# Strassen output projection of a gated MLP: when a sum, a load and a weight part take their turn

## The chip, the core and the metric

The kernel runs on one core of a Trainium2 chip. The core has five engines that each work through their own instructions in order: PE (matrix products; PEld is its loading of the stationary operand), DVE (elementwise work), ACT (activation functions and copies), POOL and SP. In the part of the kernel that matters here SP does nothing but issue DMA transfers between the chip's memory (HBM) and the on-chip memory (SBUF). An instruction waits on semaphores of other engines or of DMAs, and everything behind it on its engine waits with it.

The metric is the device time of one execution in microseconds (us), the median of several.

## The reference

One input x of 2048 tokens by 576 features goes through a layer norm and then two branches, and the result is `x + s * silu(B)`:

```python
xn = _layernorm(x)
s = _A_ref(xn, wqkv, wo)          # sliding-window attention, 32 heads, window 256
# B: a gated MLP with a mixing of tokens
z  = gelu(xn @ w_in)              # 2048 x 4608, split into z1 and z2
z2 = _layernorm(z2)
g  = w_sp @ z2 + b_sp             # 2048 x 2048 times 2048 x 2304
B  = (z1 * g) @ w_out             # 2048 x 2304 times 2304 x 576
return x + s * silu(B)
```

Everything is float32. The change lies in the last line but one, the product `(z1 * g) @ w_out`, and in what closes it (`silu`, the product with s, the sum with x, the store).

## The kernel before

The kernel first does the layer norm, the attention, `s` and z1, z2, then the big product with `w_sp`, and at about 1652 us of its span begins the product with `w_out`. This last part is called the output stage here.

**Halves.** A float32 product is made of three passes: each operand is halved into a high part, a copy in the type fp32r (`act.activation(hi, src, Copy)`, line 115, on ACT), and a low part, what is left (`dve.tensor_tensor(lo, src, hi, subtract)`, line 116, on DVE). The passes are high times high, high times low, low times high. So a product can begin when the high half is there, and its third matmul needs the low half. The helper is `split`.

**Tiles.** The left matrix y = z1 * g, kept transposed in memory as `y_d` (2304 x 2048), is cut into four quadrant blocks a11, a12, a21, a22: first index for the token half, second for the feature half. A row pair p (0 to 7) takes 128 tokens of each token half; one block is 1152 features x 128 tokens, a tile of 128 x 1152, loaded from `y_d` in one DMA of 576 KB. The four blocks have fixed places: a11 and a21 in the tile `zr`, a22 and a12 in the tile `u2` (the profile writes it `u`). Blocks of the next pair are loaded over those of this one once their last reader is done.

**Products.** Pair 0 is computed plainly (`first_pair`: four blocks, two products each, 216 matmuls). Pairs 1 to 7 use Strassen's scheme in Winograd's form, seven products of 27 matmuls (128 x 288 out of 128 x 128 blocks): P1 = a11 B11, P2 = a12 B21, P3 on what is left in a12 with B22, P4 = a22 with the weight sum T4, P5 on the sum in a22 with T1, P6 on the sum in a11 with T2, P7 on the sum in a21 with T3. The list `SEQ` has the order: P4 P1 P6 P2 P5 P7 for pair 1, and then, pair by pair, P4, P1, P3 of the pair before, P6, P2, P5, P7.

**Operand sums.** Four sums in place, on DVE, make the Winograd operands. They are called A to D here: A, line 1325, a22 = a21 + a22; B, line 1326, a21 = a11 - a21; C, line 1328, a11 = a22 - a11; D, line 1330, a12 = a12 - a11. `y_form` halves the block of a product into one of three operand tiles `o0`, `o1`, `o2` and then runs the sums that belong there: A and B behind P4's block, C behind P1's, D behind P2's.

**Turns.** After product i `formed(i + 3)` halves the operand of product i + 3, whose tile product i has just left free, and `y_load` fetches a block of the next pair over it where that block is no longer read: a11 behind P2, a22 behind P5, a21 behind P7, a12 behind P3. A pair's result is closed twice, behind P7 and behind P3, by `finish`: `sv = sv * silu`, `xr = xr + sv` (lines 1500 and 1501), the store of `xr` to `out`, and then `load_end`, which loads the rows of s (`sv`) and of x (`xr`) for the next closing. Each of these has one buffer, so the next `xr` is loaded when the store has read the last one to its end.

**Weights.** `w_out` has 63 blocks of 128 x 288 for the scheme (B11, B21, B22, B12, T4, T2, T1, nine each), in 13 tiles of five. `w_fetch(i)` loads part i (720 KB; two loads where a tile spans two of the matrices), `w_halve(i)` halves it. Parts 0 to 6 come before the stage, 7 to 12 (tiles b5, w0, w1, w2, w3, w4; w4 has three blocks) in its first products. T3 is put where B12 was, in three parts (`t3_fetch`, `t3_halve`), since pair 0 needs B12 and no other T3. Raw parts lie in two buffers `wr` in turn.

**The start.** While pair 0 runs, the last gate products z1 * g (six multiplications, line 1358, and six stores to `y_d`, 256 KB each) are run off from a list called `lazy`; the memory they used (`wk`) is then closed and a new pool `yp` opened in it for w2 to w4, `sv`, `xr` and others, so these wait for the six stores.

**Order.** In this part the kernel is under a manual schedule: each engine's instructions stand in the order in which the code calls them. So the order of lines in the loop over `SEQ` is the order on SP, DVE and ACT.

Of the kernel before, what the change touches and what calls it, by code (L numbers as in the profile page):

```python
# [64 lines left out]
def kernel(  # L65
# [1142 lines left out]
    with ExitStack() as ph:  # L1208
# [108 lines left out]
        def y_form(i):  # L1317
            p, prod = SEQ[i]
            home = yw if i % 3 < 2 else homes["o2"]
            o = home.tile([P, 2304], F32R, name=f"o{i % 3}", bufs=1).rearrange("p (a f t) -> p a f t", a=2, t=P)  # L1320
            q = {name: quads.get((p, name)) for name in QUAD_AT}
            split(o[:, 0], o[:, 1], q[OF.get(prod, prod)])
            operands[p, prod] = o
            if prod == "P4":
                dve.tensor_tensor(q["a22"], q["a21"], q["a22"], ALU.add)
                dve.tensor_tensor(q["a21"], q["a11"], q["a21"], ALU.subtract)
            if prod == "P1":
                dve.tensor_tensor(q["a11"], q["a22"], q["a11"], ALU.subtract)
            if prod == "P2":
                dve.tensor_tensor(q["a12"], q["a12"], q["a11"], ALU.subtract)  # L1330
# [155 lines left out]
        def load_end():  # L1486
            if row_order:
                r = end_rows(*row_order.pop(0))
                t = [yp.tile([P, D], F32, name=n, bufs=1) for n in ("sv", "xr", "gs")]
# [63 lines left out]
        def formed(i):  # L1553
            if i < len(SEQ):
# [3 lines left out]
                if p == 0 or (p < LAST and prod in after_):  # L1558
                    y_load(p + 1, prod if p == 0 else after_[prod])

        for i, (p, prod) in enumerate(SEQ):
            if p == 0:
                first_pair(i, prod)
                if i == 0:
                    w_halve(8, right, "w0")
                    w_fetch(9, right)
                    w_fetch(10, right)
                    y_load(1, "a12")
# [3 lines left out]
                    y_load(1, "a11")  # L1572
                    y_load(1, "a21")
                    load_end()
                    w_halve(9, right, "w1")
                formed(i + 3)
# [3 lines left out]
                if i == 1:  # L1580
                    w_fetch(11, right)
                    w_halve(10, yp, "w2")
                    finish()
                    w_fetch(12, right)
                    w_halve(11, yp, "w3")
                if i == 2:
                    t3_fetch(right, T3_PARTS[0])
                    w_halve(12, yp, "w4")
                if i == 3:
                    finish()  # L1590
                    t3_fetch(right, T3_PARTS[1])
                    t3_halve(T3_PARTS[0])
                    t3_fetch(right, T3_PARTS[2])
                    t3_halve(T3_PARTS[1])
                    t3_halve(T3_PARTS[2])
# [4 lines left out]
            formed(i + 3)  # L1600
            if prod in ("P7", "P3"):
# [77 lines left out]
```

## Time and profile before

| what | value |
|---|---|
| time of 3 runs | median 1920.37 us (1917.13 to 1921.77) |
| profiled execution | 1926.44 us, of which span 1924.4 us and 2.0 us around it |
| granted TensorE clock, mean of the span | 0.985 |
| PE busy in the span | 1844.4 us (96%) |
| DVE, ACT busy in the span | 1139.1 us (59%), 945.1 us (49%) |
| first matmul of the output stage to the end of the span | 1652.4 to 1924.4 us, 272 us |

The profiled execution is 6.1 us longer than the median of the runs; everything taken from the trace is in its time. The profile counts a matmul as busy to its modelled end, so PE's share says little; waits and the starts of matmuls say more. DMA issues stand under SP (written SPq): a row's time is that of the issue. When a transfer has landed is seen from what waited for it. In the rows `o` is an operand tile, `w` and `b` are weight tiles, `c` a PSUM bank of the output stage.

### The profile page before, as it was taken

The numbers are of one execution on the slowest core, as the hardware profiler recorded it, in microseconds if no ns is written. First come the engines' busy times: TensorE is split into PE (matmuls) and PEld (weight loads), VectorE is DVE, ScalarE is ACT, GpSimd is POOL, SyncE is SP. The second block draws the span as 40 slices with busy tenths as digits, with TensorE's granted clock in tenths as the row PEclk, the third lists the DMA queues.
The fourth block names the chain that finished last, engine by engine and source line by source line (L and its number), as shares of the span: only waits on it lengthen the run. The fifth ranks groups of instructions, "written<-read, shape, count | busy, mean of one in ns | idle before, by whom it ended". The sixth has DMA issues, their size and how long they took to land.

```text
span 1924.4 us, 38178 instructions
## 1 busy us (share of the span) xinstructions
PE 1844.4 (96%) x14363; PEld 1604.9 (83%) x14363; DVE 1139.1 (59%) x2289; ACT 945.1 (49%) x1758; POOL 432.2 (22%) x507
## 2 busy tenths in 40 slices
PE   8999999999999999999999999999999999969887
PEld 8999999997777677777988788888888888868887
DVE  6321334467666777632267877679765777456666
ACT  5432223325666576666476655555545444233232
POOL 3232333343555455554000000212000000000000
PEclk9999999999999999999999999999999999979999
DMA  7885698786666666646777777887775567733444
GB/s 254 200 233 147 228 306 287 261 256 184 171 189 182 158 187 187 183 124 198 248 253 243 233 243 238 294 297 258 258 251 179 187 200 255 238 116 121 138 125 123
DMA packets 266920, 405.75 MB, mean 211 GB/s; under 512 B 52336, under 2 KB 180592, under 8 KB 266608
## 3 DMA queue, kind: packets, MB, share of 16 engines
q1 hardware_dynamic: 266736, 403.32, 68.1%
q8 instruction: 113, 1.85, 0.4%
q14 instruction: 71, 0.58, 0.1%
HBM read 285.35 MB, written 117.09 MB: 209 GB/s over the span
## 4 chain that ended last, share of the span: by engine, by line
PE 69%; DMA 11%; DVE 11%; ACT 3%; SPq 3%; issue 2%; POOL 0%; DVEq 0%; ACTq 0%; POOLq 0%
PE acc L1428 31%; PE mb L206 11%; PE ma L671 6%; PE mb L671 5%; PE ops L752 4%; PE ma L206 4%; PE tps L724 3%; DMA u<-y_d 2%; PE sp L600 2%; DVE o L116 2%; SPq L363 1%; ACT o L115 1%; DMA s_d<-so 1%; DMA zr<-y_d 1%; DMA out_dram<-xr 1%
## 5 line engine op out<-in xcount | busy, mean ns | idle before, releaser
L1428 PE MATMUL acc<-spl,zh 128*128 128x512 f32 x1008 | 393.4, 390 | 2.3 <-DVE spl L116 2.0
L1428 PE MATMUL acc<-sph,zh 128*128 128x512 f32 x1008 | 393.0, 390 | 0.8 <-ACT sph L115 0.8
L1428 PE MATMUL acc<-sph,zl 128*128 128x512 f32 x1008 | 392.9, 390 | 0.0
L604 DVE CUSTOM_DVE_ANT_0 junk<-sp,band 128x384 bf16<-128x384 f32 (+1 forms) x512 | 276.2, 539 | 116.2 <-PE sp L600 30.2
L728 ACT ACTIVATE pt<-tps 128x384 f32<-128x384 f32 (+2 forms) x576 | 231.3, 441 | 122.8 <-PE tps L724 77.7
L116 DVE TENSOR_TENSOR spl<-spr,sph 128x1024 fp32r<-128x1024 f32 x168 | 208.7, 1242 | 39.6 <-ACT sph L115 38.6
L671 PE MATMUL mb<-b,z1wh 64*128 64x512 f32 x648 | 225.6, 401 | 2.7 <-ACT z1o L676 2.2
L671 PE MATMUL ma<-b,z1wh 64*128 64x512 f32 x648 | 224.8, 399 | 0.6 <-ACT zt L948 0.4
L1428 PEld LDWEIGHTS acc<-spl,zh 128*128 128x128 f32 x1008 | 189.4, 188 | 43.2 <-DVE spl L116 4.3
L1428 PEld LDWEIGHTS acc<-sph,zh 128*128 128x128 f32 x1008 | 189.3, 188 | 40.6 <-ACT sph L115 1.2
L1428 PEld LDWEIGHTS acc<-sph,zl 128*128 128x128 f32 x1008 | 189.4, 188 | 38.8
L1519 PE MATMUL c<-b,o 128*128 128x288 f32 x1056 | 158.5, 311 | 35.6 <-DVE o L116 23.1
L115 ACT ACTIVATE zh<-b 128x384 fp32r<-128x384 f32 x168 | 87.4, 520 | 208.0 <-PE acc L1428 205.2
L1519 PEld LDWEIGHTS c<-b,o 128*128 128x128 f32 x1056 | 152.4, 202 | 39.6 <-DVE o L116 26.4
L115 ACT ACTIVATE sph<-spr 128x1024 fp32r<-128x1024 f32 x168 | 176.0, 1048 | 14.0 <-DMA spr<-sc_d 8.6
L724 PE MATMUL tps<-att 56*128 56x384 f32 (+1 forms) x576 | 177.7, 346 | 2.4 <-DMA att<-mhl 1.8
L116 DVE TENSOR_TENSOR zl<-b,zh 128x384 fp32r<-128x384 f32 x168 | 100.8, 600 | 127.1 <-ACT zh L115 116.8
L600 PE MATMUL sp<-att 54*128 54x384 f32 (+1 forms) x512 | 162.0, 351 | 3.2 <-DVE mx L604 3.0
L671 PE MATMUL ma<-b,z1wl 64*128 64x512 f32 x324 | 128.4, 396 | 0.0
L671 PE MATMUL mb<-b,z1wl 64*128 64x512 f32 x324 | 128.0, 395 | 0.0
L949 DVE BATCH_NORM_STATS2 st<-zt 128x6 f32<-128x384 f32 x96 | 49.3, 548 | 131.3 <-ACT zt L948 131.0
L724 PEld LDWEIGHTS tps<-att 56*128 56x128 f32 x576 | 99.8, 184 | 31.0 <-issue 9.4
(214 smaller groups left out, 4206.8 us busy)
## 6 DMA issues: line engine op xcount, KB each, us to landing
spr<-sc_d SPq DMA_DIRECT2D x96, 512.0 KB
spr<-in_w_sp_dram SPq DMA_DIRECT2D x72, 512.0 KB
zr<-z_d SPq DMA_DIRECT2D x144, 192.0 KB
z_d<-zt SPq DMA_DIRECT2D x48, 384.0 KB
z_d<-z1o SPq DMA_DIRECT2D x72, 256.0 KB
z1t<-z_d SPq DMA_DIRECT2D x72, 256.0 KB
y_d<-z1t SPq DMA_DIRECT2D x72, 256.0 KB
a<-in_w_sp_dram SPq DMA_DIRECT2D x64, 256.0 KB
```

The lines of the kernel that those rows point to most:

```text
L115: act.activation(hi, src, AF.Copy)
L116: dve.tensor_tensor(lo, src, f32(hi), ALU.subtract)
L206: pe.matmul(banks[h][:, :n], *both[h][i], start=i == 0, stop=i == STEPS - 1)
L600: pe.matmul(ps[:, :w], q_of(u, j)[0:54, i * P:(i + 1) * P], k_of(u, j)[0:54, k0:k0 + w], start=True, stop=True)
L604: dve.tensor_tensor_reduce(out=junk[:, :w], in0=ps[:, :w], in1=band[:, m0:m0 + w], scale=1.0, scalar=-3.0e38, op0=ALU.add, op1=ALU.max, ac ...
L671: pe.matmul(ps, w, x_, start=n == 0, stop=n == STEPS - 1)
L724: pe.matmul(ps[:, :m * P], k_of(u, j)[:, (kb - base) * P:(kb - base + 1) * P], q_of(u, j)[:, (a - lo) * P:(a - lo + m) * P], start=True, s ...
L728: act.activation(pt[:, j, d0:d0 + n * P], ps[:, (qa - a) * P:(qa - a + n) * P], AF.Exp, scale=scale)
L752: pe.matmul(o_ps[c][32 * j:32 * j + 32, (qa - 4 * c) * P:(hi - 4 * c + 1) * P], vgs[u][:, kb - k0, j * VW:j * VW + 32], pt[:, j, (qa - kb) ...
L949: dve.bn_stats(st2[:, s, pc, :], zv)
L1428: pe.matmul(acc[j], z[:, ps], w[:, cs], start=s == i == 0 and n in OPENS, stop=s == 7 and i == 2, skip_group_check=True)
L1519: pe.matmul(banks[key][:, :288], y, w, start=begin and k == n == 0, stop=close and k == 8 and n == 2, skip_group_check=True)
```

## The change

- In `y_form` the sums A and B move from behind P4's low half to behind P1's low half, ahead of C.
- `xr` has two buffers instead of one.
- At the start, the loads of a11 and a21 of pair 1 move on SP from behind the six gate stores to ahead of weight part 9. Halving the operand of product 3 and the load of a22 of pair 1 move to ahead of the stores. Part 10 is fetched behind four of the stores, and a12 of pair 1 behind `sv` and `xr`. The halving of w1 goes behind that of product 3's operand.
- Halvings of weight parts and T3 parts each come one or more products later: w3 in product 2, w4 in product 3, the T3 parts behind products 5, 6 and 7.

The same instructions run, with the same shapes.

```diff
@@ y_form
-            if prod == "P4":
+            if prod == "P1":
                 dve.tensor_tensor(q["a22"], q["a21"], q["a22"], ALU.add)
                 dve.tensor_tensor(q["a21"], q["a11"], q["a21"], ALU.subtract)
-            if prod == "P1":
                 dve.tensor_tensor(q["a11"], q["a22"], q["a11"], ALU.subtract)
@@ load_end
-                t = [yp.tile([P, D], F32, name=n, bufs=1) for n in ("sv", "xr", "gs")]
+                t = [yp.tile([P, D], F32, name=n, bufs=1 + (n == "xr")) for n in ("sv", "xr", "gs")]
@@ formed
-                if p == 0 or (p < LAST and prod in after_):
-                    y_load(p + 1, prod if p == 0 else after_[prod])
+                if i == 3 or (p < LAST and prod in after_):
+                    y_load(p + 1, "a22" if i == 3 else after_[prod])
@@ the loop over SEQ, pair 0
                 if i == 0:
+                    y_load(1, "a11")
+                    y_load(1, "a21")
                     w_halve(8, right, "w0")
                     w_fetch(9, right)
+                formed(i + 3)
+                if i == 0:
+                    run_lazy(6)
+                    w_halve(9, right, "w1")
                     w_fetch(10, right)
-                    y_load(1, "a12")
                     run_lazy(len(lazy))
                     gates.close()
                     yp = open_pool(ph, "yp")
-                    y_load(1, "a11")
-                    y_load(1, "a21")
                     load_end()
-                    w_halve(9, right, "w1")
-                formed(i + 3)
+                    y_load(1, "a12")
...
                     finish()
+                if i == 2:
                     w_fetch(12, right)
                     w_halve(11, yp, "w3")
-                if i == 2:
                     t3_fetch(right, T3_PARTS[0])
-                    w_halve(12, yp, "w4")
                 if i == 3:
                     finish()
+                    w_halve(12, yp, "w4")
                     t3_fetch(right, T3_PARTS[1])
-                    t3_halve(T3_PARTS[0])
-                    t3_fetch(right, T3_PARTS[2])
-                    t3_halve(T3_PARTS[1])
-                    t3_halve(T3_PARTS[2])
                 continue
...
             formed(i + 3)
+            if i == 5:
+                t3_halve(T3_PARTS[0])
+                t3_fetch(right, T3_PARTS[2])
+            if i in (6, 7):
+                t3_halve(T3_PARTS[i - 5])
```

Two places show how the order on an engine changes. First SP at the start of the output stage, before; `wr` is a raw weight part (5x288 is a whole part; `4x288` and `288` are the two loads of part 10), `zr<-y_d` is a11 or a21 of pair 1, the first `u_15526<-y_d` a12 and the second a22:

```order
L1274 DMA wr<-t_d 128x5x288 x2
L1274 DMA wr<-t_d 128x4x288
L1274 DMA wr<-t_d 128x288
L1315 DMA u_15526<-y_d 128x9x128
L1364 DMA y_d<-z1t 128x512 x6
L1315 DMA zr<-y_d 128x9x128 x2
L1490 DMA sv<-s_d 128x576
L1491 DMA xr<-in_x_dram 128x576
L1315 DMA u_15526<-y_d 128x9x128
L1274 DMA wr<-t_d 128x5x288
```

And with the change, where the first `u_15526<-y_d` is a22 and the second a12:

```order
L1274 DMA wr<-t_d 128x5x288
L1315 DMA zr<-y_d 128x9x128 x2
L1274 DMA wr<-t_d 128x5x288
L1315 DMA u_15526<-y_d 128x9x128
L1363 DMA y_d<-z1t 128x512 x4
L1274 DMA wr<-t_d 128x4x288
L1274 DMA wr<-t_d 128x288
L1363 DMA y_d<-z1t 128x512 x2
L1489 DMA sv<-s_d 128x576
L1490 DMA xr<-in_x_dram 128x576
L1315 DMA u_15526<-y_d 128x9x128
L1274 DMA wr<-t_d 128x5x288
```

a11 and a21 pass part 9, part 10, a12 and six stores; a22 passes part 10, six stores, `sv` and `xr`; a12 falls behind all of these.

Second, DVE at the turn of a pair, before; `o<-u` is the low half of P4's block, `o<-zr` that of P1's, `u3s` the first of the three small sums behind P7:

```order
L116 TENSOR_TENSOR o_22110<-u_15526,o_22110 128x1152
L1325 TENSOR_TENSOR u_15526<-zr,u_15526 128x1152
L1326 TENSOR_TENSOR zr<-zr 128x1152
L116 TENSOR_TENSOR o_22143<-zr,o_22143 128x1152
L1328 TENSOR_TENSOR zr<-u_15526,zr 128x1152
L1539 TENSOR_TENSOR u3s<-c_22049,t_22000 128x288
```

And with the change:

```order
L116 TENSOR_TENSOR o_22110<-u_15526,o_22110 128x1152
L116 TENSOR_TENSOR o_22141<-zr,o_22141 128x1152
L1325 TENSOR_TENSOR u_15526<-zr,u_15526 128x1152
L1326 TENSOR_TENSOR zr<-zr 128x1152
L1327 TENSOR_TENSOR zr<-u_15526,zr 128x1152
L1538 TENSOR_TENSOR u3s<-c_22049,t_22000 128x288
```

The low half of P1 stands ahead of A and B instead of behind them; the three sums A, B, C still stand ahead of `u3s`. (Line numbers of the changed kernel are one lower up to the loop over `SEQ`.)

## The prediction

> **What bounds the kernel now.** I read the table by stages first, then PE's waits in the output stage, then the instructions of each engine in time, to see who is late for whom. The waits, from 1490 us to the end:
>
> ```profile
> PE c L1519 <- DVE o L116: 26.2, 17, 4.3
> PE c L1519 <- ACT o L115: 8.8, 3, 5.6
> PE c L1519 <- ACT t L1534: 6.1, 1, 6.1
> ```
>
> PE loses 41.1 us to late operand halves, all behind 1681 us; the big product before them waits for next to nothing and is untouched. They come in two kinds. PE at the start of the stage:
>
> ```profile
> 1652.39 28.75 PE L1519 MATMUL c<-b,o 128*128 128x288 f32 x216
> 1686.76 0.85 PE L1519 MATMUL c<-b,o 128*128 128x288 f32 x2 [5.61 <-ACT o L115]
> ...
> 1696.80 3.58 PE L1519 MATMUL c<-b,o 128*128 128x288 f32 x25 [2.99 <-DVE o L116]
> 1702.85 0.85 PE L1519 MATMUL c<-w,o 128*128 128x288 f32 x2 [2.47 <-ACT o L115]
> 1704.25 5.83 PE L1519 MATMUL c<-w,o 128*128 128x288 f32 x25 [0.55 <-DVE o L116]
> 1716.18 0.85 PE L1519 MATMUL c<-b,o 128*128 128x288 f32 x2 [6.11 <-ACT t L1534]
> ...
> 1723.36 3.73 PE L1519 MATMUL c<-w,o 128*128 128x288 f32 x27
> 1726.92 5.31 PE L1519 MATMUL c<-b,o 128*128 128x288 f32 x39
> 1732.07 2.15 PE L1519 MATMUL c<-w,o 128*128 128x288 f32 x15
> ```
>
> From 1723.36 to 1726.92 an undisturbed product takes 3.56 us. Pair 0 (28.75) ends at 1681.14; six products of pair 1 and P4 of pair 2 would be through 7 x 3.56 later, at 1706.1. They were through at about 1734.1: 28 us lost, some 18 in waits and 10 in slow matmuls (25 of them in 5.83 us instead of 3.58).
>
> Why the first wait: ACT stood 18 us for a22 of pair 1, whose load SP issued only at 1677.33, behind weights, stores and the other blocks; it landed 8.2 us later, in a stretch in which the DMAs were full.
>
> ```profile
> 1677.33 0.38 SPq L1315 DMA_DIRECT2D u<-y_d  x1
> ...
> 1685.54 1.16 ACT L115 ACTIVATE o<-u 128x1152 fp32r<-128x1152 f32 x1 [18.18 <-DMA u<-y_d]
> ```
>
> The same stretch in the table by stages (last columns: granted clock, DMA share, GB/s):
>
> ```profile
> 1660.00:1668.00 8.00, 8.00 (x62) 8.00 (x62) 7.23 (x10) 3.03 (x3) 0.00 (x0) 1.00 0.59 183
> 1668.00:1676.00 8.00, 8.00 (x63) 8.00 (x62) 1.26 (x1) 0.00 (x0) 0.00 (x0) 1.00 1.00 318
> 1676.00:1684.00 8.00, 5.14 (x39) 4.91 (x38) 0.00 (x0) 0.00 (x0) 0.00 (x0) 1.00 1.10 318
> ```
>
> At 1660 to 1668 the DMAs were 0.59 busy, DVE nearly full; then the DMAs were full and DVE and ACT empty.
>
> From pair 2 on there is a rhythm. DVE from one turn of pairs to the next:
>
> ```profile
> 1791.26 1.36 DVE L1325 TENSOR_TENSOR u<-zr,u 128x1152 f32<-128x1152 f32 x1 [3.10 <-DMA zr<-y_d]
> ...
> 1796.59 0.45 DVE L1539 TENSOR_TENSOR u3s<-c,t 128x288 f32<-128x288 f32 x1
> ...
> 1799.59 1.36 DVE L116 TENSOR_TENSOR o<-u,o 128x1152 fp32r<-128x1152 f32 x1 [1.56 <-ACT o L115]
> ...
> 1811.22 1.36 DVE L116 TENSOR_TENSOR o<-u,o 128x1152 fp32r<-128x1152 f32 x1 [1.57 <-ACT o L115]
> ...
> 1814.33 1.35 DVE L116 TENSOR_TENSOR o<-zr,o 128x1152 fp32r<-128x1152 f32 x1
> 1818.24 1.36 DVE L116 TENSOR_TENSOR o<-u,o 128x1152 fp32r<-128x1152 f32 x1 [2.57 <-ACT o L115]
> 1822.67 1.36 DVE L1325 TENSOR_TENSOR u<-zr,u 128x1152 f32<-128x1152 f32 x1 [3.07 <-DMA zr<-y_d]
> 1824.07 1.36 DVE L1326 TENSOR_TENSOR zr<-zr 128x1152 f32<-128x1152 f32 x1
> 1825.34 1.35 DVE L116 TENSOR_TENSOR o<-zr,o 128x1152 fp32r<-128x1152 f32 x1
> 1826.73 1.36 DVE L1328 TENSOR_TENSOR zr<-u,zr 128x1152 f32<-128x1152 f32 x1
> 1828.01 0.45 DVE L1539 TENSOR_TENSOR u3s<-c,t 128x288 f32<-128x288 f32 x1
> ```
>
> The low halves are those of P3 (1799.59), P2, P5, P7, P4 (1818.24) and P1 (1825.34). SP and ACT beside it:
>
> ```profile
> 1800.98 0.37 SPq L1315 DMA_DIRECT2D u<-y_d  x1
> ...
> 1805.34 1.17 ACT L115 ACTIVATE o<-u 128x1152 fp32r<-128x1152 f32 x1 [3.24 <-DMA u<-y_d]
> ...
> 1812.61 0.37 SPq L1315 DMA_DIRECT2D u<-y_d  x1
> 1814.07 0.35 SPq L1502 DMA_DIRECT2D out_dram<-xr  x1
> ...
> 1817.70 0.33 SPq L1491 DMA_DIRECT2D xr<-in_x_dram  x1
> 1818.09 0.43 SPq L1315 DMA_DIRECT2D zr<-y_d  x1
> ```
>
> and SP's waits of this kind, summed (us, times, longest):
>
> ```profile
> SPq L1491 <- DMA out_dram<-xr: 36.2, 15, 3.8
> ```
>
> Followed link by link this is a closed loop in which PE has no part: u3s 1796.59, its SiLU, P3's halves, the load of a12 (issued 1800.98, landed 1805.34), P2's halves, D, the sum and SiLU behind P3, P5's halves (low 1811.22), the closing of a pair, the store of `out`, the wait of 3.2 us for it in front of `xr`, the load of a21 behind that (issued 1818.09, landed 1822.6), A, B, P1's low half, C, u3s at 1828.01. It takes 31.42 us, while seven products need 7 x 3.56 = 24.9. PE's waits of 3.2 us at P1 and its slow matmuls there only fill the difference. First and last turn of this kind:
>
> ```profile
> 1733.67 0.45 DVE L1539 TENSOR_TENSOR u3s<-c,t 128x288 f32<-128x288 f32 x1
> ...
> 1891.99 0.45 DVE L1539 TENSOR_TENSOR u3s<-c,t 128x288 f32<-128x288 f32 x1
> ```
>
> Five rounds, 158.3 us, 31.66 each.
>
> **The loop after the change.** With a second `xr` buffer the load of `xr` no longer waits for the store, so a21 can be issued as soon as P7's low half is through: 1814.33 + 1.35, say 1815.7 instead of 1818.09. At the same 4.54 us it lands at 1820.2. That wait hides another: the load of a22 (1812.61) lands at 1817.05, then P4's low half begins at 1818.24. What is late next is this path. Behind P4's low half now stands P1's (1.28 later, by the pitch 1826.73 to 1828.01), then A at 1820.8; a21 is there 0.6 us earlier. A and B take 1.39 each (1824.07 less 1822.67), C 1.28: u3s at 1824.85. The round is 28.26 instead of 31.42, 3.16 less: 1.87 since A begins earlier, 1.28 since the low half is out from between A and u3s. Behind A, B and C on DVE wait u3s, P3's low half and P6's; they gain the 3.16 with them. P1's low half itself comes 5.8 us earlier (1819.52 against 1825.34), so PE's wait there goes; PE will wait at P3 instead, whose low half ends 4.4 us after u3s.
>
> Against 158.3 us five rounds of 28.26 are 141.3: **17.0 us**. The chain cannot be shorter unless its own members are. It can be longer: the transfer of `xr` (288 KB) now runs beside a22 and a21. I take 0.25 us for each of the loop's two loads, the spread of the rows here (4.36 to 4.54 us), five rounds: **minus 2.5**. Bound on the bad side: both loads at 1 us more, minus 10; on the good side nothing.
>
> **The start after the change.** a11 and a21 of pair 1 pass weight part 9 on SP, and with it all that stood ahead of them. This is what was in flight from 1652 to 1690 us:
>
> ```profile
> DMA packets 9138, 8.24 MB, mean 217 GB/s; under 512 B 304, under 2 KB 8112, under 8 KB 9136
> ```
>
> At the 318 GB/s of the full stretch it takes 25.9 us from the stage's begin, to 1678.3; the reordered start moves the same bytes. Part 11 (0.74 MB, 2.3 us) comes last; I take 1680.5 for it and 1676 for all before it. Then DVE's chain, step by step, with 1.28 to 1.36 for an operand half, 1.39 for a sum (rows above), 1.6 for a weight part:
>
> ```profile
> 1662.70 1.66 DVE L116 TENSOR_TENSOR w<-wr,w 128x1440 fp32r<-128x1440 f32 x1
> ```
>
> - w0's low half (this row) ends at 1664.3, that of product 3 now follows and ends at 1665.6: a22 is issued at 1665.7, 11.6 us earlier, and lands by 1673.9 even at 8.2 us. P4's halves end by 1676.5, wanted at 1681.1: the wait of 5.6 and the 0.55 behind it go, with 4.6 us to spare.
> - w2 (part 10, ACT 1.4, DVE 1.6) ends at 1679, the first closing at 1680.5, P1's low half at 1681.9 (wanted 1684.7: the 2.99 goes), A, B, C at 1686, w3 at 1687.6, P6's low half at 1689 (wanted 0.4 us sooner). This is what moving w3's and w4's parts behind the operands is worth: w3 no longer stands ahead of P1's half.
> - The next closing ends at 1690.5, w4 (three blocks, about 1.1) at 1691.6, P2's low half at 1693 (wanted 0.3 sooner), D at 1694.4, P5's at 1695.7 (in time). The 2.47 and 6.11 shrink to these tenths. The T3 parts, which stood ahead of P2's half, come behind P5's half and later ones, each beside a running product.
> - a22 of pair 2 is issued at 1695.8 and lands at 1700.2 (4.44 as at 1812.61); T3's first part, a small sum and P7's low half end at 1698.6, a21 lands at 1703.2; P4's low half ends at 1702.8, T3's last part at 1703.2, P1's low half at 1704.6, A, B, C at 1708.6. So the first turn's u3s falls at 1708.5 instead of 1733.67: **25.2 us**.
>
> PE alone would allow 28 (above), the bound on the good side; the 10 us of slow matmuls are in it, as they followed the waits. On the bad side w2, w3 and w4 each land 3.7 us later (8.2 against 4.5 us, what a22's load lost in the full stretch) and each holds the operand half behind it on ACT: 11 less, 14 us. I stay near the good end since from 1679 on DVE sets the steps, not the DMAs; for the forecast's own range I allow one part late, 21.5.
>
> **The end.** The last loads of `xr` wait for a store too; the last closing but one pays for it:
>
> ```profile
> 1919.43 0.46 DVE L1501 TENSOR_TENSOR xr<-xr,sv 128x288 f32<-128x288 f32 x1 [1.23 <-DMA xr<-in_x_dram]
> ```
>
> That goes: **1.2**.
>
> **Sum.** 17.0 - 2.5 + 25.2 + 1.2 = 40.9. The profiled execution had 1926.44 us (span 1924.4): 1885.5. The median is 6.1 lower, and nothing in the trace says where, so I take the same gain off it: 1920.37 - 40.9 = **1879.5**. Its own range by the bounds: at best 17 + 28 + 1.2 = 46, 1874; at worst 17 - 10 + 21.5 + 1.2 = 30, 1890.
>
> **Rivals.**
> 1. *PE becomes the bound by its clock.* Behind waits of 2.47 and 0.55 us, 25 matmuls took 5.83 us, but behind 2.99 only 3.58. In the new rhythm a wait of about 2.4 us remains at P3: P5 goes from 1812.6, P7, P4 and P1 follow to 1826.8, and P3's low half ends at 1824.85 + 4.36 = 1829.2. One slow product per round (2.25 us) still fits: 24.9 + 2.25 is under 28.26. Two, and the half of that wait, make some 30: five rounds then give 8 instead of 14.5, time 1886. [...] Chance 0.06.
> 2. *Weights starve the start.* The bad end above: 14 instead of 25.2, time 1891. For it: each weight half on ACT stands ahead of an operand half. Against: DMAs at 0.59 in front of 1668. Chance 0.10.
> 3. *The loop only changes its wait.* If a21 takes the 8.2 us seen in the full stretch, A begins at 1823.9, the round is 31.4, and with 1.5 from it only start and end remain: 28, time 1892. Against: in the pairs the DMAs are not full. Chance 0.08.
> 4. *The change doesn't do what it says:* `xr` is still held, by some other semaphore, and the start by DVE; no difference, 1920. Chance 0.02.
> 5. *Slower.* A stands now at a place where u3s, P3's, P6's halves and the a12 load all queue behind a21. Each us by which a21 lands later than 5.1 us after its issue is paid in every round. Without the start's gain it turns slower from 5.1 + 3.4 = 8.5 us on, with all of it from 5.1 + 40.9/5 = 13.3; at 14, 1923. The longest such load here took 8.2. Chance 0.02.
>
> My forecast keeps 0.72. **Range** 1873 to 1895: it holds the forecast's own range (1874 to 1890) and rivals 1 to 3 nearly whole. A change under 0.3% (5.8 us) cannot be told from none here. Faster 0.96, same 0.02, slower 0.02.
>
> **What would show it.** PE at 1681 goes on from pair 0 into P4 without a wait; u3s first at about 1708.5 and then every 28.3 to 28.8 us; DVE's wait in front of A gone or under 0.5; SP's waits of `xr` for `out` gone; PE's wait moved from P1 to P3. A round of 31 would show rival 3, 30 with slow matmuls rival 1, waits for w2 to w4 on ACT rival 2. I'm wrong if the start's gain is under 15 us or the round over 30.

## The result and the profile after

The changed kernel takes 1888.1 us (median of 4 runs, 1882.5 to 1895.2), the kernel before 1919.4 us beside it (1917.1 to 1921.8): ratio 0.9839, 95% interval 0.9803 to 0.9875. That is 31.3 us faster. The forecast was 40.9 us faster, 1879.5 us; the time lies in the range, and the gain is three quarters of the forecast's.

The two profiled executions differ by more, 1924.4 against 1880.5 us of span. The part before the output stage took 1652.4 us in the one and 1640.0 in the other, and in the changed kernel and its variants below it lay anywhere from 1640.0 to 1652.2 us, so this is no effect of the change. I therefore compare from the first matmul of the stage:

| us | before | after | gain | forecast |
|---|---|---|---|---|
| first matmul to the first `u3s` | 81.3 | 59.7 | 21.6 | 25.2 |
| five rounds, `u3s` to `u3s` | 158.3 | 147.8 | 10.5 | 14.5 |
| last of these `u3s` to the end of the span | 32.4 | 33.0 | -0.6 | 1.2 |
| the stage | 272.0 | 240.5 | 31.5 | 40.9 |

The stage's 31.5 us agree with the 31.3 us of the medians. All three terms are short, by 3.6, 4.0 and 1.8 us.

**PE.** Its waits after the change, by what ended them (us in total, times, longest):

```profile
PE c L1518 <- ACT o L115: 11.9, 7, 2.6
PE c L1518 <- DVE o L116: 7.5, 9, 1.0
```

They fell from 41.1 to 19.4 us. PE at the start of the stage:

```profile
1639.99 30.34 PE L1518 MATMUL c<-b,o 128*128 128x288 f32 x228
1670.17 2.15 PE L1518 MATMUL c<-w,o 128*128 128x288 f32 x15
1672.15 3.76 PE L1518 MATMUL c<-b,o 128*128 128x288 f32 x27
1677.67 0.53 PE L1518 MATMUL c<-w,o 128*128 128x288 f32 x2 [1.75 <-ACT o L115]
1679.23 4.96 PE L1518 MATMUL c<-w,o 128*128 128x288 f32 x25 [1.03 <-DVE o L116]
```

PE goes from pair 0 (216 matmuls) into P4 (12 of the first row, and the 15 of the second) and P1 without a wait; before, it lost 5.6 us there and 3.0 us behind it. What is left is P6's wait, 1.75 + 1.03 us where I had expected 0.4, and 25 slow matmuls behind it (4.96 us instead of 3.58).

**What was late in the start.** SP and ACT after the change; the `u` issued at 1653.45 is a22 of pair 1, `w<-wr` is the high half of w2, the `u` issued at 1685.56 is a22 of pair 2:

```profile
1648.20 0.36 SPq L1274 DMA_DIRECT2D wr<-t_d  x1
1653.45 0.36 SPq L1315 DMA_DIRECT2D u<-y_d  x1
...
1666.45 1.41 ACT L115 ACTIVATE w<-wr 128x1440 fp32r<-128x1440 f32 x1 [4.80 <-DMA sv<-s_d]
...
1685.56 0.36 SPq L1315 DMA_DIRECT2D u<-y_d  x1
...
1691.55 1.17 ACT L115 ACTIVATE o<-u 128x1152 fp32r<-128x1152 f32 x1 [2.63 <-DMA u<-y_d]
```

w2's high half began 26.5 us behind the stage's first matmul. My working had the whole part, low half included, done 26.6 us behind it (1679 less 1652.4); the low half ended at 29.5. a22 of pair 2 took 6.0 us from issue to use instead of 4.44. The table by stages of the changed kernel (us; busy PE, PEld, DVE, ACT, POOL; last the granted clock, DMA share, GB/s) shows the rest:

```profile
1640.00:1652.00 12.00, 12.00 (x92) 12.00 (x91) 10.43 (x13) 5.04 (x4) 0.00 (x0) 1.00 0.98 280
1652.00:1656.00 4.00, 4.00 (x32) 4.00 (x31) 4.00 (x5) 1.41 (x1) 0.00 (x0) 1.00 0.25 52
1656.00:1660.00 4.00, 4.00 (x32) 4.00 (x31) 0.54 (x2) 1.52 (x2) 0.00 (x0) 1.00 1.07 298
1660.00:1668.00 8.00, 8.00 (x63) 8.00 (x62) 1.12 (x2) 3.19 (x5) 0.00 (x0) 1.00 1.08 353
1668.00:1676.00 8.00, 7.91 (x60) 7.67 (x58) 7.90 (x7) 2.32 (x2) 0.00 (x0) 1.00 0.75 234
1676.00:1684.00 8.00, 5.30 (x27) 5.07 (x28) 7.93 (x8) 6.09 (x9) 0.00 (x0) 0.79 0.55 171
1684.00:1692.00 8.00, 8.00 (x63) 8.00 (x62) 5.80 (x6) 3.03 (x3) 0.00 (x0) 1.00 1.10 314
```

For 12 us from the stage's begin the DMAs were nearly full (0.98). Then they ran nearly empty: at 1652 to 1656 they moved 52 GB/s, and from 1656 to 1668 they were full. The reason stands on SP. Behind part 9 (1648.20) its next transfer is a22 of pair 1 (1653.45), which may overwrite its tile only when DVE has made product 3's low half. SP waited for that, and part 10, the stores and all else stand behind this load on SP (us, times, longest, from 1639 to 1672):

```profile
SPq L1315 <- DVE o L116: 4.8, 1, 4.8
```

Four us at 52 instead of 318 GB/s are 1.06 MB, or 3.3 us of a full stretch (an estimate from these two rates), close to the 2.9 us by which w2 is late. No run took this wait out, so that it is the cause is read from the trace and not tried.

DVE stood nearly empty at 1660 to 1668 (1.12 of 8 us) and then had hardly a free moment until 1684 (7.90 and 7.93 of 8). PE's clock dropped to 0.79 in the stretch of P6's wait and was back in the next.

**The rounds.** DVE after the change, one whole round and the beginning of the next:

```profile
1728.83 0.45 DVE L1538 TENSOR_TENSOR u3s<-c,t 128x288 f32<-128x288 f32 x1
...
1731.83 1.36 DVE L116 TENSOR_TENSOR o<-u,o 128x1152 fp32r<-128x1152 f32 x1 [1.56 <-ACT o L115]
...
1741.56 0.45 DVE L1545 TENSOR_TENSOR u2s<-c,u2s 128x288 f32<-128x288 f32 x1
1743.58 1.36 DVE L116 TENSOR_TENSOR o<-u,o 128x1152 fp32r<-128x1152 f32 x1 [1.57 <-ACT o L115]
...
1751.87 1.35 DVE L116 TENSOR_TENSOR o<-zr,o 128x1152 fp32r<-128x1152 f32 x1
1755.16 1.36 DVE L1325 TENSOR_TENSOR u<-zr,u 128x1152 f32<-128x1152 f32 x1 [1.94 <-DMA zr<-y_d]
...
1759.22 0.45 DVE L1538 TENSOR_TENSOR u3s<-c,t 128x288 f32<-128x288 f32 x1
```

P1's low half (1751.87) is through before A, as the change has it. A still waits for a21: 1.94 us here, 0.73 to 1.94 in the five rounds. SP in the same round; `u` is a22 of the next pair, `zr` a21:

```profile
1744.97 0.37 SPq L1315 DMA_DIRECT2D u<-y_d  x1
1746.43 0.35 SPq L1501 DMA_DIRECT2D out_dram<-xr  x1
1746.83 0.42 SPq L1489 DMA_DIRECT2D sv<-s_d  x1
1747.34 0.42 SPq L1490 DMA_DIRECT2D xr<-in_x_dram  x1
1748.06 0.37 SPq L1315 DMA_DIRECT2D zr<-y_d  x1
```

The wait of `xr` for the store is gone, and a21's load goes out as soon as P7's low half has read the tile. But it lands only at 1755.1, 7.05 us later, where 4.54 had been enough before. The five transfers are now issued within 3.1 us; before, the wait of 3.2 us had held the last two back until the first ones were through. The rounds take 29.1, 30.4, 29.1, 30.0 and 29.2 us, 29.55 in the mean, where 28.26 plus 0.5 was forecast.

**The end.** PE at P3 of pair 6:

```profile
1850.49 0.54 PE L1518 MATMUL c<-b,o 128*128 128x288 f32 x2 [1.50 <-ACT o L115]
1851.88 5.11 PE L1518 MATMUL c<-b,o 128*128 128x288 f32 x25 [0.86 <-DVE o L116]
```

PE's wait went from P1 to P3, as forecast. In the rounds it costs nothing, as the run with two passes below shows. In the last turn there is no next round to hide it: 2.36 us of waits and 1.5 us of slow matmuls (5.11 less 3.58) stand on the way to the end.

### The profile page after: what moved, and what is told of

It is laid out like the page before. It is cut to its first block, busy times and chain, and to the rows that moved or that the text cites. A ratio compares the mean times of both kernels' runs of the same rounds, so it can differ in the third digit from the quotient of the medians.

```text
span 1880.5 us, 38182 instructions
## 1 busy us (share of the span) xinstructions
PE 1830.0 (97%) x14363; PEld 1594.7 (85%) x14363; DVE 1138.0 (61%) x2289; ACT 945.7 (50%) x1758; POOL 432.5 (23%) x507
## 4 chain that ended last, share of the span: by engine, by line
PE 77%; DVE 10%; DMA 7%; ACT 3%; issue 2%; SPq 1%; POOL 0%; DVEq 0%; ACTq 0%; POOLq 0%
PE acc L1427 32%; PE ma L206 13%; PE ma L671 6%; PE mb L206 6%; PE mb L671 5%; PE ops L752 4%; PE sp L600 3%; PE tps L724 3%; PE c L1518 3%; DMA zr<-y_d 1%; DVE o L116 1%; PE wops L1157 1%; DMA u<-y_d 1%; ACT o L115 1%; DMA y_d<-z1t 1%
## 5 line engine op out<-in xcount | busy, mean ns | idle before, releaser
L604 DVE CUSTOM_DVE_ANT_0 junk<-sp,band 128x384 bf16<-128x384 f32 (+1 forms) x512 | 276.4, 540 | 114.1 <-PE sp L600 32.2
L116 DVE TENSOR_TENSOR spl<-spr,sph 128x1024 fp32r<-128x1024 f32 x168 | 209.7, 1248 | 40.3 <-ACT sph L115 39.4
L1518 PE MATMUL c<-b,o 128*128 128x288 f32 x1056 | 152.4, 304 | 15.3 <-ACT o L115 10.2
L1518 PEld LDWEIGHTS c<-b,o 128*128 128x128 f32 x1056 | 147.3, 195 | 18.4 <-ACT o L115 11.6
```

Of the source, the lines that this page charges most:

```text
L116: dve.tensor_tensor(lo, src, f32(hi), ALU.subtract)
L604: dve.tensor_tensor_reduce(out=junk[:, :w], in0=ps[:, :w], in1=band[:, m0:m0 + w], scale=1.0, scalar=-3.0e38, op0=ALU.add, op1=ALU.max, ac ...
L1518: pe.matmul(banks[key][:, :288], y, w, start=begin and k == n == 0, stop=close and k == 8 and n == 2, skip_group_check=True)
```

## The experiments

Three questions: what did each part of the change give; is the loop really a chain on ACT, DVE and the loads, and a21's landing what keeps it above 28.3 us; and what holds the start. All figures of stages are from the profiled executions; "five rounds" as in the table above.

### The three parts, each alone

A second `xr` buffer alone, on the kernel before:

```diff
-                t = [yp.tile([P, D], F32, name=n, bufs=1) for n in ("sv", "xr", "gs")]
+                t = [yp.tile([P, D], F32, name=n, bufs=1 + (n == "xr")) for n in ("sv", "xr", "gs")]
```

> The kernel before with the second xr buffer alone. Theory: in the changed kernel the load of a21 was issued at once behind P7's low half but took 5.9 to 7.0 us instead of the 4.54 us I had taken, since the transfers of out, sv, xr and a22 run beside it. Then here A begins at 1821.6 to 1822.7 in the time of the round that I quoted (before 1822.67), the round is 30.4 to 31.4 us instead of 31.7 and the time 1914 to 1919 us. Rival: the transfers do not disturb each other and a21 lands after 4.5 us; then A begins at 1820.2, the round is 28.95 us and the time 1906 us.

Measured: 1912.3 us against 1917.2, ratio 0.9975 (0.9964 to 0.9986). Five rounds 153.3 us, 30.65 each; the end 31.75 instead of 32.4. So the wait removed is worth 1.0 us a round, and not the whole of what its own size would let one hope: a21 is issued earlier and then takes longer, 5.9 to 6.6 us from issue to landing. The time came out under the expected 1914 to 1919 us.

The sums A and B behind P1's low half alone, on the kernel before:

```diff
@@ y_form
-            if prod == "P4":
+            if prod == "P1":
                 dve.tensor_tensor(q["a22"], q["a21"], q["a22"], ALU.add)
                 dve.tensor_tensor(q["a21"], q["a11"], q["a21"], ALU.subtract)
-            if prod == "P1":
                 dve.tensor_tensor(q["a11"], q["a22"], q["a11"], ALU.subtract)
```

> The kernel before with A and B behind P1's low half alone; xr still has one buffer. Theory: a21 is issued late as before (landed 1822.6), but only A, B and C stand between its landing and u3s, 4.06 instead of 5.34 us: the round falls from 31.7 to 30.3 us, the time to about 1912 us; PE's wait moves from P1 to P3. Rival: PE's wait of 3.2 us at P1 was itself the loss; then it goes, 5 x 3.2 = 16 us, and the time is 1903 us.

Measured: 1911.8 us, ratio 0.9965 (0.9952 to 0.9978). Five rounds 151.1 us, 30.2 each: 1.44 us a round, close to the 1.28 that one low half takes on DVE. So little more than the low half left the chain.

The start's order alone: the changed kernel with A and B back behind P4's low half, and one `xr` buffer:

```diff
@@ y_form, on the changed kernel
-            if prod == "P1":
+            if prod == "P4":
                 dve.tensor_tensor(q["a22"], q["a21"], q["a22"], ALU.add)
                 dve.tensor_tensor(q["a21"], q["a11"], q["a21"], ALU.subtract)
+            if prod == "P1":
...
-                t = [yp.tile([P, D], F32, name=n, bufs=1 + (n == "xr")) for n in ("sv", "xr", "gs")]
+                t = [yp.tile([P, D], F32, name=n, bufs=1) for n in ("sv", "xr", "gs")]
```

> The changed kernel without its change to the sums and with one xr buffer: only the order of loads and weight parts at the start. Theory: start and rounds are separate, so the start keeps its gain, 21 to 22 us from the first matmul of the stage to the first u3s, and the rounds are 31.4 to 31.7 us as before: time 1898 us. Rival: the second xr buffer and the later sums carry part of the start too (the first two closings lie in it); then the start gains only 15 us or so and the time is 1904 us.

Measured: 1897.5 us, ratio 0.9893 (0.9876 to 0.991). To the first `u3s` 58.8 us, rounds 31.4 to 31.6 as before the change. This is nearly the whole of the start's gain; here P6 did not wait, as A and B ran while DVE had nothing else, and instead the last T3 part came late (PE's waits from 1490 us on):

```profile
PE c L1519 <- DVE o L116: 19.2, 13, 3.3
PE c L1519 <- DVE b L116: 3.8, 1, 3.8
```

By the ratios the three parts are worth 4.8, 6.7 and 20.5 us of 1919.4, together 32.0; the whole change gave 30.9, with an interval of about 7 us to each side. By the stages of the profiles they do not add up: 6.8, 10.0 and 23.5 us are 40.3, against 31.5. The first two gave 12.3 us in the rounds by themselves and all together 10.5, and the start's share is 26.2 against 21.6. A profile is one execution, and the same kernel before stands in all three differences. So each part gave time, but an overlap of some us between them is not excluded.

### Is a21's landing what keeps the rounds above 28.3?

On the changed kernel, `sv` and `xr` of the closing behind P3 are loaded after a21 instead of ahead of it:

```diff
+        due = []
+
-        def finish(c0=0, c1=D):
+        def finish(c0=0, c1=D, now=True):
...
-                load_end()
+                if now:
+                    load_end()
+                else:
+                    due.append(1)
@@ the loop over SEQ
             formed(i + 3)
+            if due:
+                due.pop()
+                load_end()
...
-                    finish()
+                    finish(now=p == LAST or prod == "P7")
```

> The changed kernel with the loads of sv and xr behind P3's closing issued one turn later, behind the load of a21. Theory: a21 was slow because sv and xr (576 KB together) stood ahead of it in the same queue; now it lands in about 4.5 to 5 us, DVE's wait in front of A (0.7 to 1.9 us) is gone or under 0.2, the round is 28.3 to 28.5 us instead of 29.1 to 30.4 and the time 5 us under that of the changed kernel, 1883 us. Rival: a21 is slow because of the store of out and of a22 ahead of it; then it stays near 5.5 us, the round near 29 and the time within 2 us of the changed kernel.

SP in one round, and DVE behind it:

```profile
1750.64 0.35 SPq L1503 DMA_DIRECT2D out_dram<-xr  x1
1752.28 0.36 SPq L1315 DMA_DIRECT2D zr<-y_d  x1
1752.69 0.94 SPq L1489 DMA_DIRECT2D sv<-s_d  x1
1753.67 0.90 SPq L1490 DMA_DIRECT2D xr<-in_x_dram  x1
...
1757.68 1.36 DVE L1325 TENSOR_TENSOR u<-zr,u 128x1152 f32<-128x1152 f32 x1 [0.21 <-DMA zr<-y_d]
```

a21 lands within 5.4 us of its issue, and A's wait is 0.21 instead of 1.94. Measured: 1881.4 us, ratio 0.9807 (0.9792 to 0.9822), whose interval still touches that of the change (from 0.9803 on); the rounds say more. They take 28.23, 28.58, 28.31, 28.38 and 28.36 us: the 28.26 of the forecast, within 0.3. How long DVE stood idle in front of A, in all rounds, in four kernels (us, times): a second `xr` buffer alone,

```profile
  DMA zr<-y_d: 11.9, 5
```

the sums alone,

```profile
  DMA zr<-y_d: 9.9, 5
```

the whole change,

```profile
  DMA zr<-y_d: 5.8, 5
```

and with the loads behind a21:

```profile
  DMA zr<-y_d: 0.5, 2
```

The 5.3 us between the last two are most of the 5.9 us by which the five rounds shrank. So the chain had been read rightly, and one member of it was sized wrongly.

### Has PE a part in the rounds?

On the changed kernel, one of the three passes (high half of y times low half of the weights) is left out in pairs 1 to 7, so these products are computed less exactly, and PE has 7 x 9 matmuls or 8.3 us (7 x 3.56 / 3) less to do in each round:

```diff
@@ product
                 for n, (y, w) in enumerate(((o[:, 0, k], wh), (o[:, 0, k], wl), (o[:, 1, k], wh))):
+                    if n == 1 and not isinstance(key, str):
+                        continue
```

> The changed kernel without one of the three passes of every Strassen product (high half of y times low half of the weights is left out, in pairs 1 to 7): PE's work in a round is 16.6 instead of 24.9 us, all else is as it was. Theory: PE and its clock have no part in the chain, so the rounds stay at 29.1 to 30.4 us; only the products of the start's and the last pair's open ends are shorter: 1874 to 1882 us in all. Rival: PE's slow matmuls (25 in 5.1 instead of 3.6 us) hold part of the round; then it falls towards 27 us or lower and the time to 1865 us or less.

Measured: 1882.1 us, ratio 0.9816 (0.9781 to 0.985), which overlaps the interval of the change itself. Five rounds 146.3 instead of 147.8 us. PE and its waits in the rounds, first this kernel in the table by stages:

```profile
1702.00:1848.00 146.00, 104.47 (x643) 95.02 (x641) 97.45 (x101) 49.13 (x65) 0.00 (x0) 0.91 0.46 142
```

and the changed kernel:

```profile
1700.00:1848.00 148.00, 133.76 (x956) 130.96 (x955) 97.94 (x102) 49.18 (x65) 0.00 (x0) 0.97 0.46 141
```

PE is busy 29 us less in five rounds, though at a mean clock of 0.91 instead of 0.97, and the rounds take 1.5 us less. PE and its clock do not set the rounds.

### What else can leave the chain?

In the profile of the changed kernel above, `u3s` at 1728.83 and P3's low half at 1731.83 are 3.0 us apart, `u2s` at 1741.56 and P5's low half at 1743.58 2.0 us: small sums and their SiLU that run ahead of an operand only because the code has them ahead. On the changed kernel, the operand first behind P7 and P3:

```diff
             c = product(o, (p, BANK_OF[prod]), W_OF[prod])
-            sum_up(p, prod, c)
-            formed(i + 3)
+            if prod in ("P7", "P3"):
+                formed(i + 3)
+                sum_up(p, prod, c)
+            else:
+                sum_up(p, prod, c)
+                formed(i + 3)
```

> The changed kernel, with the halving of product i + 3's block put ahead of the small sums and SiLU behind P7 and P3 (before it stood behind them on DVE and ACT). Theory: the rounds of 29.1 to 30.4 us are a chain on ACT, DVE and DMA, and between C and P3's low half lie 3.0 us of small sums and SiLU, between D and P5's low half 2.0 us. Taken out, the chain over a12 and a22 falls to 23.3 us, under PE's 24.9; the chain over a21 with its landing of about 5.9 us is left and gives 25.4 to 26.4 us. Time about 1870 us. Rival: the small sums wait for products anyway, so PE or the DMAs set the round and it stays above 28.5; time 1884 us or more.

Measured: 1866.2 us, ratio 0.9728 (0.9701 to 0.9754). Five rounds 126.7 us, 25.3 each, 4.2 less than with the change. PE's waits for operand halves, 19.4 us with the change, are down to those of P6 of pair 1, 1.3 and 1.0 us; A still waits for a21, 5.5 us in all.

That and the loads behind a21 together (the two diffs above):

> Both of the two last edits on the changed kernel: sv and xr loaded behind a21, and the halves ahead of the small sums. Theory: a21 lands in about 4.5 to 5 us, its chain falls to 25 us as well, and PE's own 24.9 us is the bound: rounds 25.0 to 25.5 us, PE's waits at P3 gone, time about 1866 us. Rival: with PE pressed, another link (the a12 load behind P3, the two SiLU) holds the round at 27 us or more: time 1873 us or more.

Measured: 1866.7 us, ratio 0.9725 (0.9698 to 0.9752). Five rounds 123.8 us, 24.8 each, and A waits no more. The rounds in the table by stages:

```profile
1714.40:1838.20 123.80, 123.43 (x935) 123.23 (x934) 97.69 (x101) 50.70 (x65) 0.00 (x0) 1.00 0.55 168
```

PE is busy for 123.43 of 123.80 us. Here PE is the bound, at the 7 x 3.56 = 24.9 us that the prediction gave for it. That the medians of the two do not differ though the rounds do (2.9 us in five) stays unexplained: in its profile the start took 1.8 us longer than the other's, and 3 us are inside both intervals.

### What holds the start?

Part 10 (w2) on SP ahead of the first four gate stores instead of behind them, on the changed kernel:

```diff
                 formed(i + 3)
                 if i == 0:
+                    w_fetch(10, right)
                     run_lazy(6)
                     w_halve(9, right, "w1")
-                    w_fetch(10, right)
                     run_lazy(len(lazy))
```

> The changed kernel with weight part 10 fetched ahead of the four gate stores instead of behind them. At the start, w2's high half came 26.5 us behind the first matmul of the stage, 3 us later than I had worked out, and P6 waited 2.8 us on what stood behind it. Theory: w2 lies in memory that the stores must have left, and the DMAs are full from 16 us on, so whichever of part 10 and the stores comes last ends at the same time: w2 is not earlier by more than 1 us and the time is within 2 us of the changed kernel. Rival: part 10's place in the queue was the delay; then w2's half comes 2.5 us or more earlier, P6's wait goes and the time is 3 to 4 us lower.

ACT in this kernel, whose stage began at 1645.4:

```profile
1670.56 1.41 ACT L115 ACTIVATE w<-wr 128x1440 fp32r<-128x1440 f32 x1 [4.26 <-DMA xr<-in_x_dram]
```

Measured: 1885.9 us, ratio 0.9832 (0.9804 to 0.9859), the change's own. w2's high half began 25.2 us behind the first matmul, 1.3 earlier than with the change and 0.8 earlier than in any other kernel here with the changed start (26.0 to 26.5). P6's waits fell to 0.50 + 1.02 us, and its 25 matmuls took 3.59 us. Still the first `u3s` came at 59.6, as with the change: a22 of pair 2 was issued 1.3 us earlier and landed at the same place, 51.5 us behind the first matmul, after 7.2 us instead of 6.0. So part 10's place behind the stores is not what the first `u3s` waits for. Its place behind the load of a22 of pair 1 was not changed: here too SP waited 4.8 us for DVE, and the DMAs ran nearly empty at that point (0.32 busy, 90 GB/s, 12 to 16 us behind the first matmul).

A and B of pair 1 alone go back behind P4's low half, where DVE stood empty; on the kernel with the operands first:

```diff
@@ y_form
-            if prod == "P1":
+            if prod == ("P4" if p == 1 else "P1"):
                 dve.tensor_tensor(q["a22"], q["a21"], q["a22"], ALU.add)
                 dve.tensor_tensor(q["a21"], q["a11"], q["a21"], ALU.subtract)
+            if prod == "P1":
                 dve.tensor_tensor(q["a11"], q["a22"], q["a11"], ALU.subtract)
```

> The kernel with the halves ahead of the small sums (e5_early), and for pair 1 alone A and B back behind P4's low half, where DVE stands idle for 6.8 us before w2. For pairs 2 to 7 they stay behind P1's. Theory: at the start the changed place of A and B costs 2.7 us, since DVE is full from w2 on; with them in the idle time P6's wait (1.3 + 1.0 us, and 25 matmuls in 5.0 instead of 3.6) goes, and with PE as the bound of all that follows the stage is 3 to 4 us shorter: 212 to 213 instead of 216.0 us, time about 1863 us. Rival: the load of a22 of pair 2 (6 us from issue to landing) sets the first turn; then the stage gains under 1.5 us and the time stays within 2 us of 1866.

PE in its start:

```profile
1678.63 4.06 PE L1519 MATMUL c<-w,o 128*128 128x288 f32 x27
...
1694.09 0.40 PE L1519 MATMUL c<-b,o 128*128 128x288 f32 x1 [0.47 <-ACT b L115]
1695.52 2.12 PE L1519 MATMUL c<-b,o 128*128 128x288 f32 x14 [1.03 <-DVE b L116]
```

P6 (27 matmuls at 1678.63) has no wait; the last T3 part has one of 0.47 + 1.03 us. Measured: 1863.2 us, ratio 0.9729 (0.9705 to 0.9752); the first `u3s` 1.3 us earlier than without this edit, the stage 0.7 us shorter. These differences are no larger than those between profiles of kernels with one and the same start (60.3 and 62.2 us to the first `u3s` with the operands first and with both edits). Of P6's 2.4 us of waits (1.3 and 1.0 without this edit) and 1.4 us of slow matmuls (4.99 us less 3.58) little or nothing arrives. My reading is that behind the start the chain through a21 decides (A waits 5.9 us in all); the next run is the test of it.

The three edits together (loads behind a21, operands first, A and B of pair 1 in the empty stretch). In the expectation e6_both is the kernel with the first two, e9_hole the one just above:

> e6_both with A and B of pair 1 back behind P4's low half: all edits that helped. In e9_hole P6's wait went but the stage was only 0.7 us shorter, because the chain over a21 (A waited 0.9 to 1.5 us for it) set rounds of 25.3 to 25.7 us. Theory: with sv and xr behind a21 the rounds are PE's 24.9 us again, so the start's gain stays: the first u3s 59 us behind the stage's first matmul, rounds 24.5 to 25.0, stage 212 to 213.5 us, time about 1862 us. Rival: another wait of the start (T3's last part, 1.5 us in e9_hole) grows in its place; then the stage stays at 215 us.

Measured: 1863.3 us against 1917.2, ratio 0.9718 (0.9701 to 0.9735), the best ratio of all, though not apart from the three others with the operands first. The stage takes 213.9 us, 1.8 less than without the third edit, which is again no more than profiles of one and the same start differ by. The rounds take 24.5 to 25.7 us, and in three of them A waits for a21, 2.5 us in all; so the chain through a21 has not left altogether. PE's waits in the stage:

```profile
PE c L1524 <- DVE b L116: 1.6, 2, 1.0
PE c L1524 <- DVE o L116: 0.8, 1, 0.8
PE c L1524 <- DVE u3s L1546: 0.4, 1, 0.4
PE c L1524 <- ACT b L115: 0.2, 1, 0.2
```

3.0 us are left of 41.1. Pair 0 and 49 products at 3.56 need 28.75 + 174.4 = 203.2 us, so at the pace of an undisturbed product no order of these instructions can take more than another 10.7 us from the stage, and part of that is the last closing behind the last matmul.

| kernel | median us | ratio (95%) | stage | to first u3s | five rounds | to the end |
|---|---|---|---|---|---|---|
| before | 1919.4 | | 272.0 | 81.3 | 158.3 | 32.4 |
| the change | 1888.1 | 0.9839 (0.9803-0.9875) | 240.5 | 59.7 | 147.8 | 33.0 |
| second `xr` alone | 1912.3 | 0.9975 (0.9964-0.9986) | 265.2 | 80.2 | 153.3 | 31.75 |
| sums alone | 1911.8 | 0.9965 (0.9952-0.9978) | 262.0 | 78.7 | 151.1 | 32.2 |
| start alone | 1897.5 | 0.9893 (0.9876-0.991) | 248.5 | 58.8 | 157.5 | 32.25 |
| change, loads behind a21 | 1881.4 | 0.9807 (0.9792-0.9822) | 235.4 | 60.5 | 141.9 | 33.0 |
| change, operands first | 1866.2 | 0.9728 (0.9701-0.9754) | 216.0 | 60.4 | 126.7 | 28.9 |
| both of these | 1866.7 | 0.9725 (0.9698-0.9752) | 215.7 | 62.2 | 123.8 | 29.7 |
| change, two passes | 1882.1 | 0.9816 (0.9781-0.985) | 239.0 | 60.75 | 146.3 | 32.0 |
| change, part 10 earlier | 1885.9 | 0.9832 (0.9804-0.9859) | 237.8 | 59.6 | 146.8 | 31.4 |
| operands first, A and B of pair 1 early | 1863.2 | 0.9729 (0.9705-0.9752) | 215.3 | 59.1 | 127.4 | 28.8 |
| all three | 1863.3 | 0.9718 (0.9701-0.9735) | 213.9 | 59.9 | 124.5 | 29.4 |

The ratios are against runs of the kernel before that were made beside each kernel (its medians there were 1917.0 to 1920.6 us). The last four columns are single profiled executions. With the operands first, `u3s` stands behind P3's low half on DVE, so there the columns "to first u3s" and "to the end" are cut at another place.

## Why the prediction was right, and where it was not

**The reading of the bound was right.** PE's waits are filler, and the loop is a chain on ACT, DVE, SP and the loads in which PE has no part: with a third of PE's work in the pairs taken away, the rounds lost 0.3 us each. The removed wait for the store was in the chain, the low half was in it, and the start's loads were a part of their own; each alone gave time.

**The loop: the step that failed is "At the same 4.54 us it lands at 1820.2 … a21 is there 0.6 us earlier", with its "minus 2.5" for contention.** a21 took 5.85 to 7.05 us in the changed kernel, and A waited 0.73 to 1.94 us in every round, 5.75 in five. I had seen the transfer of `xr` come beside a21's, and sized it by a spread of 0.18 us in rows where SP's wait had kept the transfers apart; that cover went with the wait. The allowance of 0.5 a round should have been 1.3 (29.55 less 28.26). The size without it was right: with the loads behind a21 the rounds take 28.2 to 28.6 us. "Both loads at 1 us more, minus 10", the bad bound, held: the rounds lost 6.4 of the 17.0.

**The start: the step that failed is "I take 1680.5 for it and 1676 for all before it".** It rested on bytes at the full rate of 318 GB/s from the stage's begin on. But the list behind it has a22 of pair 1 issued only 13.3 us behind that begin, when DVE is through with product 3's low half, and SP issues in order: part 10 and the stores wait behind it. The prediction gave that wait no price. SP stood 4.8 us, the DMAs ran nearly empty (52 GB/s at 1652 to 1656), and w2 was through at 29.5 us instead of 26.6. From then on DVE works through the chain as the prediction lists it, 2.2 to 2.9 us late, and that is P6's wait. What the table by stages shows beside it is, on DVE, an empty stretch at 1660 to 1668 and a full one behind: A and B of pair 1, moved by the change with all others, left the empty one for the full one. The variant that has them back (and the one with the start alone) has no wait at P6, but a later one at T3's last part. The rest of the start's 3.6 us is a22 of pair 2, "4.44 as at 1812.61": it took 6.0 in a stretch with the DMAs at 1.10 and 314 GB/s. In the run with part 10 earlier it was issued sooner and landed no sooner (7.2 us), so this load, and not the time at which w2 comes, sets the first `u3s` there. That the gain of 21.6 us falls on the 21.5 allowed for "one part late" is in part luck: that allowance was for a slow transfer and not for SP's wait or this load.

**The end: "That goes: 1.2" failed.** The wait itself shrank from 1.2 to 0.2 us; the time did not follow. A second buffer alone gave 0.7 of it. In the whole change PE's wait, moved to P3, and the slow matmuls behind it stand at a place where PE is the bound, and took 1.3 us back (0.7 to -0.6). They do not always come: in the run with part 10 earlier, whose end has the same instructions, the waits were 0.76 + 0.86 us, the 25 matmuls took 3.58, and the end 31.4, a gain of 1.0. With the operands first that wait goes, and the end takes 28.8 to 29.7 us.

**Rivals.** 1, PE's clock: not in the rounds, as the run with two passes shows, but slow products stand at P6 of pair 1 and at the end, with 1.4 and 1.5 us (granted clock 0.69 and 0.66 there); the first cost nothing that can be seen at the first `u3s`, since without it (part 10 earlier) that came no sooner. 2, weights starving the start: in part, 3.6 us lost where it gave 11; it showed as a wait of ACT for w2, of 4.8 us. 3, the loop only changing its wait: in part, a21 at up to 7.05 of its 8.2 us. 4 and 5 did not occur.

**What was to show it.** PE goes on at the end of pair 0 without a wait: yes. SP's waits of `xr` for `out` gone: yes. PE's wait from P1 to P3: yes. DVE's wait in front of A under 0.5: no, 0.73 to 1.94. First `u3s` at 1708.5, 56.1 us behind the first matmul: no, 59.7. Rounds of 28.3 to 28.8: no, 29.1 to 30.4, and one of them past the 30 at which I called myself wrong.

## What to carry to other kernels

When PE waits once in every round, follow the round link by link and write down what each engine does between two equal instructions: here a chain of ACT, DVE and loads set 31.4 us where PE needed 24.9, and a member taken off the chain gave about its own duration (1.4 us for a low half of 1.28, 4.2 for small sums of 5.0) until PE became the bound; a wait of 3.2 us gave 1.0, since the load behind it then took longer. A wait that is removed may have kept transfers apart: price the load behind it with everything that will now be issued just ahead of it, not by its duration in the old rhythm, and issue what is needed last behind what is needed next. Before counting bytes at a full rate, look on the issuing engine for a transfer that must wait: all behind it waits too, and here the DMAs ran nearly empty over it. Small sums and activations that close a result belong behind the halving of the next operand: that order alone, not a part of this change, gave 4.2 us a round.

## What the runs showed of the hardware

- The time from issue to landing of one and the same 576 KB load went from 4.54 us (in the kernel before, issued 5.5 us behind a22's and 0.4 behind that of `xr`, 288 KB) to 5.85 to 7.05 us (four transfers issued in the 3.1 us ahead of it), though the DMAs were 0.75 busy and not full at 1748 to 1755 us; with two of the four behind it, it was at most 5.4 us. With the operands first as well, in the last kernel, it was up to 6.7 us even so. How the DMA engines share their time between the transfers was not measured.
- Matmuls were slow behind some short pairs of waits. In the changed kernel, behind waits of 1.50 + 0.86 us, and of 1.75 + 1.03, 25 matmuls took 5.11 and 4.96 us, at a granted clock of 0.66 and 0.69; behind 1.19 + 0.86 us they took 3.59, at 1.00. The length of the waits alone does not decide it. In the kernel with a second `xr` buffer alone 0.71 + 0.86 us were followed by 5.11 us at one turn and by 3.56 at the next:

```profile
1817.61 0.53 PE L1519 MATMUL c<-b,o 128*128 128x288 f32 x2 [0.71 <-ACT o L115]
1819.00 5.11 PE L1519 MATMUL c<-b,o 128*128 128x288 f32 x25 [0.86 <-DVE o L116]
...
1848.77 0.53 PE L1519 MATMUL c<-b,o 128*128 128x288 f32 x2 [0.71 <-ACT o L115]
1850.16 3.56 PE L1519 MATMUL c<-b,o 128*128 128x288 f32 x25 [0.86 <-DVE o L116]
```

  With the sums alone, 25 matmuls took 3.57 us behind 1.98 + 0.87 us, and behind the single wait of 2.99 us in the prediction's rows 3.58, at a granted clock of 1.00. What does decide was not tried.
